# New ranks for the first 267 operations of a fused attention and feed-forward kernel, and the third block's loads behind the weights

## The chip, the cores and the metric

The kernel runs on one core of one Trainium2 chip. The metric is the time on the device in microseconds (us); several runs are made and their median is taken. One further execution was recorded by the hardware profiler, and everything that is read from a profile is read from that one.

## The reference

Linear attention, followed by a feed-forward layer with a sigmoid form of GELU. q, k and v are 8 x 8 x 576 x 64 (batch, heads, positions, width of a head); x has 4608 rows of 512; the weights are 512 x 2048 and 2048 x 512, handed over as 64-bit floats.

```python
q_s = exp(q - max(q, axis=-1)); q_s /= sum(q_s, axis=-1) + 1e-9
k_s = exp(k - max(k, axis=2));  k_s /= sum(k_s, axis=2) + 1e-9
kv  = einsum('bhsd,bhse->bhde', k_s, v)
x   = einsum('bhsd,bhde->bhse', q_s, kv)      # rows: batch and position, columns: head and width
h   = x @ w_in
out = (h / (1 + exp(-1.702 * h))) @ w_out
```

## The kernel before, in words

**Blocks.** The 4608 rows are cut into 12 blocks of 384 rows. A batch has 576 rows, so a block covers parts of one or two batches. For each block the kernel makes x (512 x 384, turned), then 16 steps j of the feed-forward part: `g1` multiplies 128 columns of w_in with x (12 products), ScalarE applies the GELU, and `g2` adds the result times 128 rows of w_out into three banks (three times three products). Each operand is held as a high part and a remainder (`h` and `l`), and three products replace one. The remainders (`xl`, `gl`, and the `l` half of a weight) are VectorE's work.

**Weights.** Each of 16 + 16 weight tiles (wi0 to wi15, wo0 to wo15, 512 KB each) is loaded once as 64-bit words and converted in place by `conv_w`: ScalarE scales the upper word (c1), VectorE shifts the lower word (c2, line 255), puts the words together in two integer steps (c3, lines 259 and 260), ScalarE casts the high part (c5, line 264) and VectorE subtracts it (c6, line 270). Three scratch tiles `tmp` go round, so that a conversion can begin only when the third one before it is done. The converted weights stay for all blocks.

**Attention.** For a new batch: `k_max` (VectorE, lines 397 to 399, then a maximum over partitions on GpSimd), `k_sub` (line 418, then the exponential on ScalarE), `kv_pairs` (products of k and v, then a division). For a block: `q_soft` (maximum and subtraction, lines 502 and 503; exponential, line 506; sum and division, lines 509 to 512), `q_tr` (turns q), `x_pairs` (q times kv) and `x_out` (high part on ScalarE, remainder xl on VectorE, line 547). Batches 0 and 1 are worked in two groups of four heads (i = 0, 1). For these two the inputs lie in the storage of weight tiles that are loaded later (`held`): the queries of batch 1, for example, in that of wi14 and wi15; such a weight's load waits until they are read.

**Steps.** Block 0 and block 1 share the weights as these come in: block 1's steps stand 9 ranks (`JOIN`) behind those of block 0. From block 2 on blocks follow each other, and the next block's attention lies between the steps of the one before.

**The order.** Nothing is ordered by hand. Every operation is handed to `Plan.add` with its engine, a cost in us, what it reads and writes, and a rank. `Plan.order` plays the plan through: whenever an engine is free, it takes, of the operations whose inputs are there by the estimates, the one with the lowest rank; it never leaves an engine idle for a better one. The program is written in the order in which the operations began there, and each engine then runs its own instructions in this order. All loads are issued on SyncE's queue. A load of so many bytes is expected by these lines:

```python
free[e] = done = now + cost
if size:
    wire = max(wire, done) + size / self.RATE
    done = wire + self.LAND
```

where `wire` is one line shared by all loads, `RATE` is in bytes per us, and `LAND` in us. `ISSUE` is the cost of an issue on SyncE.

Of the kernel before, what the change touches and what calls it, by code (L numbers as in the profile page):

```python
# [18 lines left out]
class Plan:  # L19
# [1 line left out]

    HOP, LAND, RATE, ISSUE, TABLE = 0.1, 1.8, 270e3, 0.5, 1.28

    def __init__(self):
        self.ops = []
# [19 lines left out]
    def order(self):  # L47
        ops = self.ops
        left = [len(o[2]) for o in ops]
        users = [[] for _ in ops]  # L50
        for n, o in enumerate(ops):
            for d in o[2]:
                users[d].append(n)
        engines = sorted({o[0] for o in ops})
        free = dict.fromkeys(engines, 0.0)
        ready = {e: [] for e in engines}
        coming = []
        at = [0.0] * len(ops)
        for n, o in enumerate(ops):
            if not left[n]:  # L60
                heapq.heappush(ready[o[0]], (o[3], n))
        wire, table = 0.0, None
        began = []
        self.start = {}
        now = 0.0
        while len(began) < len(ops):
            while coming and coming[0][0] <= now:
                _, n = heapq.heappop(coming)
                heapq.heappush(ready[ops[n][0]], (ops[n][3], n))
            moved = False  # L70
            for e in engines:
                if free[e] > now or not ready[e]:
                    continue
                _, n = heapq.heappop(ready[e])
                _, cost, _, _, _, needs, size = ops[n]
                if needs is not None and needs != table:
                    cost, table = cost + self.TABLE, needs
# [4 lines that stand above are left out]
                began.append(n)  # L82
                self.start[n] = now
                moved = True
                for u in users[n]:
                    left[u] -= 1
                    hop = 0.0 if ops[u][0] == e and not size else self.HOP
                    at[u] = max(at[u], done + hop)
                    if not left[u]:
                        heapq.heappush(coming, (at[u], u))  # L90
            if not moved:
                times = [f for e, f in free.items() if f > now and ready[e]]
                if coming:
                    times.append(coming[0][0])
                now = min(t for t in times if t > now) if any(t > now for t in times) else now
        return began


def dve(n, psum=False):
    return 0.15 + n / 960  # L100

# [6 lines left out]
def efficient_attention_then_gelu_ffn(  # L108
# [27 lines left out]
    ST = S - SM  # L136
    W = D + 1
    JOIN = 9

    const = ctx.enter_context(tc.tile_pool(name="const", bufs=1))  # L140
    psum = ctx.enter_context(tc.tile_pool(name="psum", bufs=1, space=bass.MemoryType.PSUM))
# [4 lines left out]
    def sb(name, shape, dtype=F32, tag=None):  # L146
        return const.tile(shape, dtype, name=name, tag=tag or name)
# [135 lines left out]
    def bc(a, n):  # L283
        return a.unsqueeze(len(a.shape)).broadcast_to([*a.shape, n])
# [4 lines left out]

    kbuf, vbuf, qbuf, tbuf = {}, {}, {}, {}  # L290

    def load_tail(b, rank):
        if b in etail:
            (kl, vl), tag = etail[b]
            keys = ((tag, 0), (tag, "v"))
        else:
            (kl, vl), keys = tail[0], ((("tail"), 0), (("tail"), 1))
        tbuf[b] = kl, vl, keys

        def run_k():  # L300
            nc.sync.dma_start(out=kl[0:ST], in_=k[b, :, SM:S, :].rearrange("h p d -> p h d"))  # L301

        def run_v():
            nc.sync.dma_start(out=vl[0:ST, :, 0:D], in_=v[b, :, SM:S, :].rearrange("h p d -> p h d"))  # L304

        plan.add("SP", plan.ISSUE, (), (keys[0],), rank, run_k, size=ST * H * D * 4)
        plan.add("SP", plan.ISSUE, (), (keys[1],), rank + 0.01, run_v, size=2 * ST * H * D * 4)

    def load_k(b, i, rank):
        n = group(b)  # L310
        t, key = ek[b, i] if b < 2 else (kt_[i], ("kt", i))
        kbuf[b, i] = t, key
        hs = slice(n * i, n * (i + 1))

        def run():
            nc.sync.dma_start(
                out=t.rearrange("p h c d -> p h (c d)"),
                in_=k[b, hs, 0:SM, :].rearrange("h (p c) d -> p h (c d)", c=CM),
            )

        plan.add("SP", plan.ISSUE, (), (key,), rank, run, size=n * SM * D * 4)

    def load_v(b, i, rank):
        n = group(b)
        t, key = ev[b, i] if b < 2 else (vt_[i], ("vt", i))
        vbuf[b, i] = t, key

        def run():
            if b < 2:
                nc.sync.dma_start(  # L330
                    out=t.rearrange("p h c d -> p h (c d)"),
                    in_=v[b, n * i : n * (i + 1), 0:SM, :].rearrange("h (p c) d -> p h (c d)", c=CM),
                )
                return
            for h in range(n):
                nc.sync.dma_start(
                    out=t[:, h, :, 0:D], in_=v[b, n * i + h, 0:SM, :].rearrange("(p c) d -> p c d", c=CM)
                )

        if b < 2:  # L340
            plan.add("SP", plan.ISSUE, (), (key,), rank, run, size=n * SM * D * 4)
        else:
            plan.add("SP", n * 0.6, (), (key,), rank, run, size=1.5 * n * SM * D * 4)

    def parts(t):

        t0 = t * TB
        b, s0 = divmod(t0, S)
        n = min(TB, S - s0)
        got = [(b, s0, 0, n // C)]  # L350
        if n < TB:
            got.append((b + 1, 0, n // C, P))
        return got
# [6 lines left out]
    def load_q(t, i, rank):  # L360
        n = group(t)
        qt, key = eq[t, i] if t < 2 else (qt_[i % 2], ("qt", i % 2))
        qbuf[t, i] = qt, key
        runs = [(0, 1, 1), (1, 0, 1)] if turned(parts(t)[0][0], i) else [(0, 0, n)]

        def run():
            for b, s0, p0, p1 in parts(t):
                for o, h, m in runs:
                    src = q[b, n * i + h : n * i + h + m, s0 : s0 + (p1 - p0) * C, :]
                    if t < 2:  # L370
                        nc.sync.dma_start(
                            out=qt[p0:p1].rearrange("p h c d -> p h (c d)"),
                            in_=src.rearrange("h (p c) d -> p h (c d)", c=C),
                        )
                    else:
                        nc.sync.dma_start(
                            out=qt[p0:p1, :, o : o + m], in_=src.rearrange("h (p c) d -> p c h d", c=C)
                        )

        plan.add("SP", plan.ISSUE * len(parts(t)) * len(runs), (), (key,), rank, run, size=n * TB * D * 4)  # L380

    nm = [0]
    maxes = {}
# [100 lines left out]

    nr = [0]
    rs = [sb(f"r{i}", [P, NP]) for i in range(2)]
    qm = [sb(f"qm{i}", [P, 4 * C]) for i in range(2)]

    def q_soft(t, i, ranks):
        n = group(t)  # L490
        qt, key = qbuf[t, i]
        M = ("qm", i % 2)
        dst, nkey = qt, key
        if t < 2:
            m = qm[i % 2].rearrange("p (h c) -> p h c", h=n)
            qn, nkey = qbuf[t, i] = en[t, i]
            dst = qn.rearrange("p c h d -> p h c d")
        else:
            m = qm[i % 2][:, : n * C].rearrange("p (c h) -> p c h", c=C)

        def run_m():
            nc.vector.tensor_reduce(out=m, in_=qt, axis=AX.X, op=ALU.max)  # L502
            nc.vector.tensor_tensor(out=qt, in0=qt, in1=bc(m, D), op=ALU.subtract)

        def run_e():
            nc.scalar.activation(qt, qt, AF.Exp)  # L506

        def run_s():
            nc.vector.tensor_reduce(out=m, in_=qt, axis=AX.X, op=ALU.add)  # L509
            nc.vector.tensor_scalar_add(m, m, 1e-9)  # L510
            nc.vector.reciprocal(m, m)
            nc.vector.tensor_tensor(out=dst, in0=qt, in1=bc(m, D), op=ALU.mult)

        e = n * C * D
        plan.add("DVE", 2 * dve(e), (key,), (key, M), ranks[0], run_m)
        plan.add("ACT", act(e), (key,), (key,), ranks[1], run_e, table="exp")
        plan.add("DVE", 2 * dve(e) + 0.35, (key,), (nkey, M), ranks[2], run_s)
# [234 lines left out]
    for rank, _, f, a in sorted(tasks, key=lambda s: s[:2]):  # L752
        if f in (load_k, load_v, load_q, k_max, k_sub, q_tr, x_pairs, g1, g2, load_w, conv_w, load_tail):
            f(*a, rank)
        else:
            f(rank)

    with tc.manual_schedule():
        for n in plan.order():
            plan.ops[n][4]()  # L760
# [24 lines left out]
```

## Time and profile before

| what | us |
|---|---|
| median of 3 runs (lowest, highest) | 916.12 (915.61, 918.11) |
| the profiled execution's own time | 916.58 |
| its span, first to last instruction | 914.7 |
| TensorE busy | 885.1 (97%) |
| VectorE busy | 390.2 (43%) |
| ScalarE busy | 487.8 (53%) |
| GpSimd busy | 27.8 (3%) |

The span is shorter than the execution's own time by what lies around the instructions. In the rows, PE is TensorE, PEld its weight loads, DVE VectorE, ACT ScalarE, POOL GpSimd and SP SyncE (SPq is its issuing of loads). L with a number is a line of the kernel. Tiles go by their names without numbers. PEclk is the TensorE clock that the chip granted, as a share of 2.4 GHz.

### The profile page before, as it was taken

How to read it: one execution, taken by the hardware profiler on the slowest of the kernel's cores; microseconds unless marked ns; L12 is line 12 of the kernel's file. 1: busy time of each engine (PE TensorE's matmuls, PEld its weight loads, DVE VectorE, ACT ScalarE, POOL GpSimd, SP SyncE). 2: the span in 40 equal slices, each digit the busy share in tenths (PEclk: the TensorE clock that was granted, in tenths of full speed). 3: DMA queues.
4: the chain of work that ended last, by engine and by line, in shares of the span. 5: the costliest groups of instructions: out<-in, count | busy, mean ns of one | idle time of the engine just before them, and what ended most of it. 6: DMA issues, size and time to landing. Idle time of an engine off the chain costs nothing.

```text
span 914.7 us, 13010 instructions
## 1 busy us (share of the span) xinstructions
PE 885.1 (97%) x5200; PEld 785.7 (86%) x5200; DVE 390.2 (43%) x826; ACT 487.8 (53%) x840; POOL 27.8 (3%) x35
## 2 busy tenths in 40 slices
PE   2879999999999999999999999999999999999998
PEld 2668989888988988989889889888988898998897
DVE  8899996162531641341541352332263134132111
ACT  3776669464952763552773583544494265253222
POOL 1100001000100100000000010000010000000000
PEclk9899999999999999999999999999999999999999
DMA  9996000111310400000400320000141000000000
GB/s 257 353 315 208 1 1 1 52 53 31 100 40 14 120 11 35 18 18 35 122 18 34 85 55 35 18 18 35 33 100 42 9 18 9 36 18 1 35 1 35
DMA packets 94620, 55.37 MB, mean 61 GB/s; under 512 B 67424, under 2 KB 87904, under 8 KB 94560
## 3 DMA queue, kind: packets, MB, share of 16 engines
q1 hardware_dynamic: 94560, 54.54, 21.0%
q8 instruction: 41, 0.67, 0.3%
q14 instruction: 19, 0.16, 0.1%
HBM read 45.09 MB, written 9.44 MB: 60 GB/s over the span
## 4 chain that ended last, share of the span: by engine, by line
PE 93%; DMA 4%; SPq 2%; DVE 1%; ACT 0%; issue 0%; DVEq 0%
PE bank L636 44%; PE bank L604 44%; PE bank L465 2%; PE bank L529 1%; PE bank L580 1%; DMA raw<-in_moe_w_out 1%; DMA raw<-in_moe_w_in 1%; DMA ek<-in_k 1%; SPq L226 0%; PE bank L575 0%; SPq L221 0%; DVE tmp L260 0%; SPq L304 0%; DVE tmp L259 0%; SPq L330 0%; SPq L301 0%
## 5 line engine op out<-in xcount | busy, mean ns | idle before, releaser
L604 PE MATMUL bank<-xh,w 128*128 128x384 f32 x1536 | 429.0, 341 | 4.6 <-ACT w L264 3.5
L636 PE MATMUL bank<-w,gh 128*128 128x512 f32 x1152 | 366.6, 399 | 0.0
L604 PEld LDWEIGHTS bank<-xh,w 128*128 128x128 f32 x1536 | 282.0, 189 | 14.7 <-ACT w L264 3.9
L616 DVE TENSOR_TENSOR gl<-g,gh 128x384 fp32r<-128x384 f32 x192 | 106.6, 556 | 385.0 <-ACT gh L613 384.3
L610 ACT ACTIVATE g<-bank 128x384 f32<-128x384 f32 x192 | 94.5, 492 | 326.8 <-PE bank L604 326.0
L604 PE MATMUL bank<-xl,w 128*128 128x384 f32 x768 | 259.7, 338 | 0.0
L636 PEld LDWEIGHTS bank<-w,gh 128*128 128x128 f32 x1152 | 214.5, 189 | 41.1 <-issue 4.4
L636 PE MATMUL bank<-w,gl 128*128 128x512 f32 x576 | 228.4, 397 | 0.0
L604 PEld LDWEIGHTS bank<-xl,w 128*128 128x128 f32 x768 | 144.9, 189 | 7.0
L636 PEld LDWEIGHTS bank<-w,gl 128*128 128x128 f32 x576 | 108.7, 189 | 25.8
L613 ACT CAST gh<-g 128x384 fp32r<-128x384 f32 x192 | 98.5, 513 | 6.3 <-PE bank L636 0.3
L610 ACT ACT_TABLE_LOAD x54 | 69.3, 1283 | 1.0
L502 DVE TENSOR_REDUCE qm<-qt 128x6 f32<-128x384 f32 x40 | 22.0, 551 | 67.2 <-DMA qt<-in_q 67.2
L506 ACT ACT_TABLE_LOAD x36 | 46.2, 1283 | 1.9 <-DMA qt<-in_q 1.3
L403 POOL PARTITION_ALL_REDUCE mx<-mx x24 | 21.0, 876 | 611.1 <-DVE mx L399 611.1
L536 ACT COPY qT<-bank 128x384 f32<-128x384 f32 x48 | 22.7, 476 | 29.8 <-PE bank L529 29.6
L509 DVE TENSOR_REDUCE qm<-qt 128x6 f32<-128x384 f32 x40 | 22.0, 550 | 25.7 <-ACT qt L506 25.6
L424 ACT ACT_TABLE_LOAD x18 | 23.1, 1283 | 5.5 <-DMA ek<-in_k 5.2
L465 PE MATMUL bank<-ev,ek 128*64 128x64 f32 x128 | 7.2, 273 | 19.0 <-ACT eq L506 12.4
L547 DVE TENSOR_TENSOR xl<-bank,xh 128x384 fp32r<-128x384 f32 x48 | 24.0, 550 | 3.0 <-ACT xh L544 3.0
L481 ACT ACTIVATE kvn<-bank,r 64x64 f32<-64x64 f32 x64 | 17.9, 306 | 14.0 <-DVE r L471 12.2
L251 ACT ACTIVATE tmp<-raw 128x512 f32<-128x512 f32 x32 | 21.2, 673 | 5.7 <-DVE w L270 5.6
(71 smaller groups left out, 495.4 us busy)
## 6 DMA issues: line engine op xcount, KB each, us to landing
out<-tmp SPq DMA_DIRECT2D x36, 256.0 KB, 2.1
raw<-in_moe_w_in SPq DMA_DIRECT2D x16, 512.0 KB, 10.0
raw<-in_moe_w_out SPq DMA_DIRECT2D x16, 512.0 KB, 10.2
kt<-in_k SPq DMA_DIRECT2D x24, 256.0 KB, 4.1
vt<-in_v SPq DMA_DIRECT2D x48, 128.0 KB, 4.0
qt<-in_q SPq DMA_DIRECT2D x36, 96.0 KB, 2.7
qt<-in_q SPq DMA_DIRECT2D x16, 192.0 KB, 2.9
ek<-in_k SPq DMA_DIRECT2D x4, 512.0 KB, 7.5
```

What stands on the lines that cost most here:

```text
L424: nc.scalar.activation(t, t, AF.Exp)
L465: nc.tensor.matmul(pk[r0 : r0 + D, m, cols], lhs, rhs, start=c == 0, stop=c == CM, tile_position=(0, r0))
L502: nc.vector.tensor_reduce(out=m, in_=qt, axis=AX.X, op=ALU.max)
L506: nc.scalar.activation(qt, qt, AF.Exp)
L509: nc.vector.tensor_reduce(out=m, in_=qt, axis=AX.X, op=ALU.add)
L536: nc.scalar.copy(qT, pq[:, :TB])
L547: nc.vector.tensor_tensor(out=xl, in0=px[:, :TB], in1=xh.bitcast(F32), op=ALU.subtract)
L604: nc.tensor.matmul(ph, wi[w][j][:, c, :], x[:, c, :], start=c == 0 and i == 0, stop=c == KC - 1 and i == 2,)
L610: nc.scalar.activation(gt, ph, AF.Gelu_apprx_sigmoid)
L613: nc.scalar.copy(gh, gt)
L616: nc.vector.tensor_tensor(out=gl, in0=gt, in1=gh.bitcast(F32), op=ALU.subtract)
L636: nc.tensor.matmul(po[c], x[:, cs], wo[w][j], start=j == 0 and i == 0, stop=j == NJ - 1 and i == 2)
```

## The change

Four edits. (1) The first 267 operations in the order of `add` with a rank under 12 get other ranks, from the table `FIRST`; all others keep theirs. The values were found by a search that played the plan through under five sets of estimates. (2) The planner's estimates of loads change: LAND from 1.8 to 2.2, RATE from 270e3 to 330e3, ISSUE from 0.5 to 0.6, and SyncE begins at 0.7. (3) `behind` makes the plan put every load of keys and values from batch 2 on, and of queries from block 2 on, behind the last write in the plan, at that point, of each tile that batch 1's inputs share with a weight. It is an order in the plan only: the buffers of these loads are others, and the chip waits for nothing more. (4) A second form of the queries' softmax with ScalarE's sums is added, for the groups named in `QACT`; the set is empty, so only its two small tiles are made.

```diff
-    HOP, LAND, RATE, ISSUE, TABLE = 0.1, 1.8, 270e3, 0.5, 1.28
+    HOP, LAND, RATE, ISSUE, TABLE = 0.1, 2.2, 330e3, 0.6, 1.28
...
-        free = dict.fromkeys(engines, 0.0)
+        free = dict.fromkeys(engines, 0.0) | {"SP": 0.7}
...
+FIRST = [
+    -3424, -9000, -8950, -8949, -8900, -8800, -8700, -8600, -8500, -8400, -8350, -8300, -8250, -8249, -8200, -8100,
+    -8000, -7900, -7800, -7899, -7123, -5395, -5792, -5064, 307, 3595, -4928, -4172, 1260, -5510, -5886, -124, 1298,
...
+]
...
+    QACT = set()
...
+    def behind(late):
+
+        return tuple((tag, 0) for tag, b in held.items() if b == 1) if late else ()
...
-        plan.add("SP", plan.ISSUE, (), (keys[0],), rank, run_k, size=ST * H * D * 4)
-        plan.add("SP", plan.ISSUE, (), (keys[1],), rank + 0.01, run_v, size=2 * ST * H * D * 4)
+        plan.add("SP", plan.ISSUE, behind(b > 1), (keys[0],), rank, run_k, size=ST * H * D * 4)
+        plan.add("SP", plan.ISSUE, behind(b > 1), (keys[1],), rank + 0.01, run_v, size=2 * ST * H * D * 4)
...
-        plan.add("SP", plan.ISSUE, (), (key,), rank, run, size=n * SM * D * 4)
+        plan.add("SP", plan.ISSUE, behind(b > 1), (key,), rank, run, size=n * SM * D * 4)
...
-            plan.add("SP", n * 0.6, (), (key,), rank, run, size=1.5 * n * SM * D * 4)
+            plan.add("SP", n * 0.6, behind(True), (key,), rank, run, size=1.5 * n * SM * D * 4)
...
-        plan.add("SP", plan.ISSUE * len(parts(t)) * len(runs), (), (key,), rank, run, size=n * TB * D * 4)
+        plan.add("SP", plan.ISSUE * len(parts(t)) * len(runs), behind(t > 1), (key,), rank, run, size=n * TB * D * 4)
...
+    sums = [sb(f"qs{i}", [P, 4 * C]) for i in range(2)]
...
+        if (t, i) in QACT:
...
+    begun = [n for n, o in enumerate(plan.ops) if o[3] < 12]
+    assert len(begun) == len(FIRST)
+    for n, r in zip(begun, FIRST):
+        e, cost, deps, _, run, table, size = plan.ops[n]
+        plan.ops[n] = e, cost, deps, r / 100, run, table, size
```

Counted off against the order of `add`, the ranks that the prediction speaks of are these (old, then new):

| operation | old | new |
|---|---|---|
| load of wi1, of batch 1's second values | -69, -78 | -78.99, -78.00 |
| load of wo3, of wi4 | -66.5, -66 | 3.07, 35.95 |
| k_max of batch 1, groups 0 and 1 | 0.4, 0.6 | -2.86, -1.23 |
| k_sub of batch 1, groups 0 and 1 | 0.5, 0.7 | -37.90, -105.52 |
| q_soft of block 1, maximum, groups 0 and 1 | 0.5, 0.7 | 0.13, -2.44 |
| q_soft of block 1, sum, groups 0 and 1 | 0.5, 0.7 | -4.46, 19.37 |
| exponentials of batch 1 and block 1 (k 0, q 0, q 1, k 1) | 0.5, 0.5, 0.7, 0.7 | -142.55, -51.56, -106.59, -78.98 |
| conversion of wi1: c2, c3, c6 | -0.2 | -73.63, -95.81, -8.94 |
| conversion of wo1: c2, c3, c6 | 0.3 | -35.20, -1.46, -58.90 |
| conversion of wi2: c2, c3, c6 | 1.8 | -4.45, -13.25, -94.43 |
| conversion of wo2: c2, c3, c6 | 2.3 | 17.40, -107.47, -51.11 |
| conversion of wi3: c2, c3, c6 | 3.8 | -33.74, -63.21, -49.11 |
| conversion of wo3: c2, c3, c6 | 4.3 | 43.23, -54.90, -1.24 |
| conversion of wi4: c2, c3, c6 | 5.8 | -82.61, 50.33, -67.93 |
| GELU of block 0, steps 0 to 3 | 0, 2, 4, 6 | -53.53, 42.80, -101.88, -48.65 |

## Rows read from the trace of the kernel before

**Rows 1.** Busy time of each engine in four stages (us from the start).

```profile
0.00:32.08 32.08, 15.43 (x180) 12.73 (x181) 25.00 (x57) 13.15 (x26) 3.64 (x10) 1.00 1.02 275
32.08:66.07 33.99, 25.13 (x247) 20.77 (x245) 31.68 (x60) 27.46 (x48) 3.17 (x2) 0.90 1.06 336
66.07:150.00 83.93, 83.93 (x414) 75.90 (x415) 79.06 (x149) 58.79 (x99) 4.08 (x4) 0.98 0.22 68
150.00:914.70 764.70, 760.64 (x4364) 676.34 (x4362) 254.45 (x564) 388.39 (x670) 16.93 (x20) 1.00 0.14 38
```

Columns of rows 1: the stretch and its length, then busy us and instructions of PE, PEld, DVE, ACT and POOL, then granted clock, share of the DMA engines, GB/s.

**Rows 2.** Timeline of TensorE from 32 to 67 us, the pieces after gaps.

```profile
36.06 0.69 PE L465 MATMUL bank<-ev,ek 128*64 128x64 f32 x16 [1.41 <-ACT ek L424]
...
39.68 0.51 PE L604 MATMUL bank<-xh,w 128*128 128x384 f32 x1 [1.11 <-ACT w L264]
...
41.14 1.01 PE L604 MATMUL bank<-xh,w 128*128 128x384 f32 x2 [0.64 <-DVE w L270]
...
52.74 0.69 PE L465 MATMUL bank<-ev,ek 128*64 128x64 f32 x16 [1.45 <-ACT ek L424]
...
65.06 0.45 PE L604 MATMUL bank<-xh,w 128*128 128x384 f32 x1 [2.42 <-ACT w L264]
...
66.07 0.62 PE L604 MATMUL bank<-xh,w 128*128 128x384 f32 x2 [0.38 <-DVE w L270]
```

Columns of a timeline: start and length in us, engine, line, operation, how many; in brackets the idle time ahead of it and what ended that.

**Rows 3.** Stretches of 2 us: TensorE's busy time and granted clock.

```profile
40.00:42.00 2.00, 1.36 (x5) 0.50 1.01 388
...
46.00:48.00 2.00, 2.00 (x9) 0.81 1.11 337
...
66.00:68.00 2.00, 1.93 (x9) 0.81 1.13 329
68.00:70.00 2.00, 2.00 (x7) 0.50 1.03 410
70.00:72.00 2.00, 2.00 (x9) 0.84 1.06 375
```

**Rows 4.** Timeline of VectorE from 30 to 66 us.

```profile
30.37 0.68 DVE L397 TENSOR_TENSOR em<-ek 128x512 f32<-128x512 f32 x1
...
37.02 0.42 DVE L255 TENSOR_SCALAR raw<-raw 128x512 uint32<-128x512 uint32 x1
37.55 0.70 DVE L259 SCALAR_TENSOR_TENSOR tmp<-tmp,raw 128x512 int32<-128x512 int32 x1
...
40.41 0.68 DVE L270 TENSOR_TENSOR w<-tmp,w 128x512 fp32r<-128x512 f32 x1
...
60.15 0.42 DVE L255 TENSOR_SCALAR raw<-raw 128x512 uint32<-128x512 uint32 x1
...
64.86 0.55 DVE L547 TENSOR_TENSOR xl<-bank,xh 128x384 fp32r<-128x384 f32 x1
65.33 0.68 DVE L270 TENSOR_TENSOR w<-tmp,w 128x512 fp32r<-128x512 f32 x1
```

**Rows 5.** Chain of waits from 0 to 75 us: two loads.

```profile
12.92 9.76 DMA ek<-in_k
...
26.76 11.87 DMA raw<-in_moe_w_out
```

**Rows 6.** Timeline of SyncE's issues.

```profile
42.04 4.36 SPq L376 DMA_DIRECT2D qt<-in_q  x2
...
73.89 3.39 SPq L226 DMA_DIRECT2D raw<-in_moe_w_out  x1
```

**Rows 7.** Timeline of VectorE: the first maximum of block 2.

```profile
134.44 0.55 DVE L502 TENSOR_REDUCE qm<-qt 128x6 f32<-128x384 f32 x1
```

**Rows 8.** What ScalarE waited for from 30 to 150 us: the longest.

```profile
ACT g L610 <- PE bank L604: 15.3, 17, 2.5
```

**Rows 9.** Timeline of ScalarE: a table load and what follows it.

```profile
36.34 1.28 ACT L610 ACT_TABLE_LOAD   x1
37.63 0.49 ACT L610 ACTIVATE g<-bank 128x384 f32<-128x384 f32 x1
```

More of the change, by code (lines that the diff above doesn't have):

```diff
@@ L514, in q_soft, with run_n, run_a, run_z @@
         e = n * C * D
+        if (t, i) in QACT:
+            flat = qt.rearrange("p h c d -> p (h c d)")
+            mf, sf = qm[i % 2], sums[i % 2]
+            def run_n():
+                nc.vector.tensor_reduce(out=m, in_=qt, axis=AX.X, op=ALU.max, negate=True)
+            def run_a():
+                for x in range(n * C):
+                    w = flat[:, x * D : (x + 1) * D]
+                    nc.scalar.activation(w, w, AF.Exp, bias=mf[:, x : x + 1], accum_out=sf[:, x : x + 1])
+            def run_z():
+                nc.vector.tensor_scalar_add(sf, sf, 1e-9)
+                nc.vector.reciprocal(sf, sf)
+                nc.vector.tensor_tensor(
+                    out=dst, in0=qt, in1=bc(sf.rearrange("p (h c) -> p h c", h=n), D), op=ALU.mult
+                )
+            Q = ("qs", i % 2)
+            plan.add("DVE", dve(e), (key,), (M,), ranks[0], run_n)
+            plan.add("ACT", 0.30 * n * C, (key, M), (key, Q), ranks[1], run_a, table="exp")
+            plan.add("DVE", dve(e) + 0.4, (key, Q), (nkey, Q), ranks[2], run_z)
+            return
         plan.add("DVE", 2 * dve(e), (key,), (key, M), ranks[0], run_m)
```

15 rows, old and new, of the table FIRST are left out of this document.

## Prediction

> **What bounds the kernel now.** I read the page first, then the busy time by stage, then each engine's timeline of the first 72 us. The four stages hold 15.43 + 25.13 + 83.93 + 760.64 = 885.13 us of TensorE work in 914.7 [rows 1], so what the change can give lies in the few stretches where it stands still. The stage table says where these are: from 66.07 us to 150 us TensorE has no idle time, and from 150 us to the end 4 us in 764.7. The first 32.08 us hold 15.43 us of busy time, the next 33.99 us hold 25.13. So 8.86 us of idle time lie between the first matmul of the feed-forward part (32.08) and 66.07, and 16.65 before it. The first part is the start of the chain: first loads, softmax of block 0, its small products. The second is where the new ranks can act most.
>
> In that second part the timeline gives the gaps one by one; the six largest that the change can touch are 1.41, 1.11, 0.64, 1.45, 2.42 and 0.38 us [rows 2]. Two of them (1.11 and 0.64) are the second step of the first layer, which waits for the conversion of wi1; the last two (2.42, 0.38) are its fourth step, which waits for wi3. Behind the gaps the granted clock falls to its lower level, 1.2 instead of 2.4 GHz [rows 3]: from 40 to 46 us it is 0.50 (the two stretches between 42 and 46 read as the one shown) and to 48 us 0.81, which costs 3 x 1.0 + 0.38 = 3.4 us, some 0.3 of which is gap counted already; from 66 to 72 us 0.81, 0.50, 0.84, that is 0.38 + 1.0 + 0.32 = 1.7. Gaps and clock make about 8.9 + 3.1 + 1.7 = 13.7 us; no more than this can come out of the second part.
>
> VectorE is what feeds it: 31.68 us busy of 33.99 [rows 1]. Its order in that time is a mix of two things [rows 4]: the softmax work of block 1 (from 30.37, last remainder x low at 64.86) and the weights' conversions. wi1 gets its first conversion step at 37.02 and its last at 40.41; wi3 its first at 60.15 and its last at 65.33.
>
> **The change, part by part.**
>
> *The planner's estimates.* The planner thought of loads as slower than they are. Up to the second key load of batch 1 it counts 5.77 MB; at 270 kB per us, plus 0.5 and 1.8, it expects that load at 23.7 us, and by the new constants (330 kB per us, plus 1.3 and 2.2) at 21.0. The chain of waits has it land at 12.92 + 9.76 = 22.68. For wo3 (10.75 MB) the two estimates are 42.1 and 36.1, and it lands at 26.76 + 11.87 = 38.63 [rows 5]. The truth lies between: the old plan was 1 to 3.5 us late, the new one is 1.7 to 2.6 us early. That matters in two ways. A late estimate makes the planner put other work first: wi1 was expected at 0.5 + 8.13/0.27 + 1.8 = 32.4, so block 1's maxima (30.37) and subtractions went ahead of it although its old rank (-0.2) stood before theirs (0.4). An early estimate puts a step in the queue ahead of work that could run while its load still travels.
>
> *wi1 earlier (gain).* Its load moves ahead of block 1's second value load, and its integer steps get ranks -73.63 and -95.81, far below block 1's maxima (-2.86) and softmax (0.13). By the new estimate it is there at 26.5. From the two landings the chip moves 4.98 MB in 15.95 us, 312 kB per us, so 7.60 MB are there at 22.68 + 1.84/0.312 = 28.6. Its steps cost on VectorE 0.42 + 0.70 + 0.70 + 0.68 [rows 4], the second integer step being as long as the first, so wi1 is whole by some 36 to 37 instead of 41.09. Then the second step of the first layer follows the first at once: the gaps 1.11 and 0.64 go, and the 1.41 ahead of them, in which TensorE had nothing else, is filled: 3.2 us. The clock's fall from 40 to 47 hangs on these gaps; but further on TensorE still waits for wi2 and for block 1, so I count half of it, 1.5. Cost: the integer steps of wi1 (0.42 + 1.40) now run ahead of the last remainders of block 0, which is 1.8 us on the first step of the first layer, and VectorE stands up to 1.0 us for the load (28.6 against the some 27.5 at which its queue gets there). Sum: 3.2 + 1.5 - 2.8 = 1.9 us gained. Bounds: 0 (the clock falls anyway, the stall is 2) to 4.7 (the clock stays, no cost on the path).
>
> *wi3 ahead of wo2, wo3 and of block 1's last softmax (gain).* Its steps get -33.74, -63.21 and -49.11; the gate of wo2 gets 17.40, that of wo3 43.23 and the last sum of block 1 (group 1) 19.37. So wi3 is converted before block 1 is ready, and the fourth step of the first layer waits no more: 2.42 + 0.38, and the fall of the clock behind it, 1.7. Sum 4.5 us. Bounds: 2.8 (the clock falls elsewhere) to 4.5.
>
> *What VectorE does ahead of block 1's end (loss).* The old order ran six whole conversions and two half ones (wi3, wo3) before 64.86. By the ranks the new one runs seven (wi0 to wi3, wo0 to wo2) and the gate of wo4 or wi4. So block 1 is ready at about the time it was, and the gaps that are filled are filled with steps of block 0 (the first layer's fourth step, 2.1, the second layer's third). After them TensorE has nothing until block 1 comes, since the last softmax sum stands so late: a new gap, taken as 1.5 (0 to 3; nearest row the 1.45 in which TensorE waits for a piece of block 1 now [rows 2]). And wi3 is planned at once on its estimated landing, which the chip misses by 1.7 to 2.6: 1.4 us of VectorE standing still (0 to 2.6), with all of block 1 queued behind it.
>
> *Third block's loads behind the weights (nothing).* These are two q, four k and eight v loads, 2.75 MB with the tails, now between the weights from 42.04 on; the last weight is issued at 73.89 [rows 6]. Behind them, they are issued at about 70 to 80 us. VectorE first needs them at 134.44 [rows 7], and no conversion after 66 us waits for a load: ScalarE, which makes each first step, waits most for TensorE (15.3 us), and what it waits for after 30 us is always another engine, never a load [rows 8]. So weights that come 8 us earlier (2.75 MB at the 336 GB/s of that stage [rows 1]) bring nothing, and the cover of some 50 us would have to go before the move costs. The edit of the planner that is not used (the set of softmax groups on ScalarE is empty) is nothing either; its two small tiles cost no time.
>
> *Table loads.* The new ranks mix the GELU of block 0 (-53.53, 42.80, -101.88, -48.65) with the exponentials of block 1 (-142.55, -51.56, -106.59, -78.98). Six table loads stand in the first 65 us now; the new order has about as many, two more at worst. One costs 1.28 us: the load starts at 36.34 and the GELU at 37.63 [rows 9]. The Trainium skill, ScalarE: Activation LUTs, section "What ACT_TABLE_LOAD costs", puts a switch at 2.66 us, a drain included, and advises to do all work of one set first; by it two more switches would cost 5.3 us. The trace shows no drain beside the 1.28 here.
>
> **Sum.** -1.9 - 4.5 + 1.5 + 1.4 = -3.5 us. The profiled execution took 916.58 us (span 914.7 and 1.88 around it), so 913.1; it lies 0.46 above the median of the runs, and on the median's scale the forecast is 916.12 - 3.5 = 912.6 us. From 0.3% (2.75 us) on a difference can be told from none here, so this is a little more than the least that counts.
>
> **Rivals.**
>
> *Nothing moves (chance 0.27, 914 to 918).* VectorE has 31.68 of 33.99 us of work [rows 1] and the change takes none of it away; if block 1's end stays and the clock falls as often, what the two gaps give is lost in the new one. For it: the same number of conversions ahead of block 1. Against: the gaps at wi1 and wi3 are of order, not of amount. Time: -1.9 - 2.8 + 3 + 2 = +0.3, so 916.4.
>
> *Loads later than the plan (slower; chance 0.15, 919 and up).* Each engine runs its instructions in the one order that the plan wrote down; each conversion that the plan starts on its estimated landing stands until the chip's. Five weights (wi1, wo1, wi2, wo2, wi3) land within this time. If all of them are met up to 2.6 us early and block 1's work stands behind, the stalls add to 5 x 1.7 = 8.5 less the 1.0 and 1.4 counted: +6.1 - 3.5 = +2.6, so 918.7. It decides once four of the five stalls lie on VectorE's path. Against it: after one stall the queue is itself late, and the next load has time.
>
> *The clock stays up (chance 0.12, 907 to 910).* If no gap over 1.5 us is left after 32 us, gaps and clock come back nearly whole: 4.7 + 4.5 - 1.4 (the stall at wi3) = 7.8, so 908.3.
>
> *Table switches (within the second-largest chance, 0.04 of its own).* Two more, 2 x 1.28 = 2.6 us on ScalarE, ahead of block 1's casts: 912.6 + 2.6 = 915.2. In a sentence by itself: by the Trainium skill's 2.66 each it would be 917.9.
>
> **Chances.** The forecast's own case (2 to 6 us faster, 910 to 914) has 0.42, the large gain 0.12, nothing 0.27 and the switches 0.04, slower 0.15. Of the forecast's case some 0.01 ends above 913.4, so faster 0.53, same 0.32, slower 0.15. The range leaves out some 0.05 below and 0.15 above: 908.5 to 918.5; the forecast's own is 910 to 914.
>
> **What the new profile would show.** Right: wi1's last conversion step before 38 us and the second step of the first layer directly behind the first; no wait for wi3 at 65; one clock fall instead of two; TensorE without gaps from some 62 to 64 us on; third block's loads issued behind the last weight with nothing waiting for them. Wrong: VectorE idle on weight loads between 27 and 40 us (the second rival), block 1's last remainder later than 66 us, more than eight table loads ahead of 65 us, or gaps after 66 us, where now there are none.

## The result: 904.8 us, and the profile of the changed kernel

The changed kernel takes 904.77 us in the median of 4 runs (903.55 to 905.83), the kernel before 915.87 (915.45 to 918.11) in the same set of runs: a ratio of 0.9869 (95%: 0.9855 to 0.9883), 11.1 us less. The profiled execution took 903.99 us, its span is 902.2. The direction was forecast, the size was not: 3.5 us were expected, and 904.77 lies below the range.

The four stages of the profile after, with the columns of [rows 1]:

```profile
0.00:32.08 32.08, 16.62 (x187) 13.84 (x187) 26.98 (x59) 15.11 (x30) 4.69 (x10) 1.00 1.02 294
32.08:66.07 33.99, 29.88 (x273) 26.09 (x273) 32.54 (x64) 25.89 (x48) 1.30 (x1) 0.90 1.07 375
66.07:150.00 83.93, 83.93 (x425) 75.93 (x424) 75.49 (x143) 58.36 (x99) 2.75 (x3) 1.00 0.17 45
150.00:902.20 752.20, 748.15 (x4320) 666.98 (x4318) 252.50 (x561) 401.95 (x677) 15.87 (x21) 1.00 0.14 39
```

Against [rows 1], TensorE's idle time went from 16.65 to 15.46 us in the first stage and from 8.86 to 4.11 in the second: 1.2 and 4.75 us. The clock of the second stage is 0.90 in both; in the third it was 0.98 and is 1.00 (84 x 0.02 = 1.7 us). Together 7.6 of the 12.5 us by which the spans differ. (The two recordings lie further apart than the medians, 12.6 against 11.1 us.) The rest doesn't come out of idle time at all; the first experiments say where it lies.

TensorE's timeline from 32 to 67 us, every piece with idle time ahead of it, answers to [rows 2]:

```profile
34.55 0.44 PE L659 MATMUL bank<-xl,w 128*128 128x384 f32 x1 [2.45 <-DVE xl L602]
...
36.77 1.12 PE L494 MATMUL bank<-ev,ek 128*64 128x64 f32 x16 [0.60 <-ACT ek L453]
...
48.46 0.87 PE L584 MATMUL bank<-ident,en 128*128 128x128 f32 x6 [0.19 <-DVE en L542]
49.58 1.57 PE L630 MATMUL bank<-qT,kvn 128*128 128x192 f32 x8 [0.24 <-ACT qT L591]
...
58.71 0.85 PE L584 MATMUL bank<-ident,en 128*128 128x128 f32 x6 [0.64 <-DVE en L542]
```

The gaps at wi1 (1.11, 0.64) and at wi3 (2.42, 0.38) are gone. One large gap is new, 2.45 us in the middle of the first layer's first step: TensorE waits there for a remainder of block 0. VectorE's timeline shows why (it answers to [rows 4]):

```profile
29.75 0.95 DVE L532 TENSOR_REDUCE qm<-eq 128x12 f32<-128x768 f32 x1
...
31.62 0.42 DVE L280 TENSOR_SCALAR raw<-raw 128x512 uint32<-128x512 uint32 x1
32.14 0.69 DVE L284 SCALAR_TENSOR_TENSOR tmp<-tmp,raw 128x512 int32<-128x512 int32 x1
32.87 0.69 DVE L285 SCALAR_TENSOR_TENSOR tmp<-raw,tmp 128x512 int32<-128x512 int32 x1
33.48 1.01 DVE L602 TENSOR_TENSOR xl<-bank,xh 128x384 fp32r<-128x384 f32 x2
...
36.82 0.67 DVE L295 TENSOR_TENSOR w<-tmp,w 128x512 fp32r<-128x512 f32 x1
...
48.32 0.42 DVE L280 TENSOR_SCALAR raw<-raw 128x512 uint32<-128x512 uint32 x1
...
51.98 0.68 DVE L295 TENSOR_TENSOR w<-tmp,w 128x512 fp32r<-128x512 f32 x1
...
63.02 1.20 DVE L602 TENSOR_TENSOR xl<-bank,xh 128x384 fp32r<-128x384 f32 x2
```

A maximum and a subtraction of block 1 (from 29.75) and then wi1's gate (its first step on VectorE, c2) and integer steps (31.62 to 33.5) stand ahead of block 0's last two remainders. wi1 is whole at 37.5. wi3's gate is at 48.32 instead of 60.15 and its last step at 51.98, ahead even of wi2's (53.05). Block 1's last remainder ends at 64.2 instead of 65.4, with eight whole conversions ahead of it (wi0 to wi3, wo0 to wo3) where the order before had six and two halves. No bracket of VectorE names a load between 6 and 66 us, and none names a weight's load in the whole run: it never stood on a weight. In the stretch from 5 to 66 us it was busy for 56.23 us (53.38 before): its idle brackets between 23 and 66 us add up to 1.5 us, where before they were 1.46, 0.87 and 0.72 up to 30 us and 0.90 and 0.26 behind.

The clock, in stretches of 2 us, answers to [rows 3]:

```profile
34.00:36.00 2.00, 1.45 (x5) 1.12 (x5) 2.00 (x5) 0.61 (x2) 0.00 (x0) 0.74 1.03 403
36.00:38.00 2.00, 1.40 (x25) 1.23 (x24) 2.00 (x4) 1.98 (x3) 0.00 (x0) 0.50 1.06 356
38.00:40.00 2.00, 2.00 (x25) 1.99 (x24) 1.63 (x5) 1.75 (x5) 0.00 (x0) 0.50 1.10 349
40.00:42.00 2.00, 2.00 (x9) 2.00 (x8) 1.93 (x5) 1.96 (x4) 0.94 (x1) 0.55 1.10 349
42.00:44.00 2.00, 2.00 (x45) 1.74 (x44) 1.97 (x3) 1.29 (x3) 0.37 (x1) 1.00 1.06 399
```

It falls once, behind the 2.45 us gap, and comes back at some 42 us after TensorE had worked on without idle time from 36.8; the second fall [rows 3] is gone, with the gap ahead of it.

On SyncE's queue the third block's loads stand behind the last weight, and block 2's first maximum ([rows 7]) is the first of VectorE's work on them:

```profile
59.59 1.12 SPq L251 DMA_DIRECT2D raw<-in_moe_w_out  x1
60.76 4.49 SPq L405 DMA_DIRECT2D qt<-in_q  x2
```

```profile
129.38 0.55 DVE L532 TENSOR_REDUCE qm<-qt 128x6 f32<-128x384 f32 x1
```

### The profile page after: what moved, and what is told of

Read it like the earlier page. It is cut to its first block, busy times and chain, and to the rows that moved or that the text cites. A ratio compares the mean times of both kernels' runs of the same rounds, so it can differ in the third digit from the quotient of the medians.

```text
span 902.2 us, 13027 instructions
## 1 busy us (share of the span) xinstructions
PE 878.6 (97%) x5200; PEld 782.8 (87%) x5200; DVE 387.5 (43%) x826; ACT 501.3 (56%) x850; POOL 24.6 (3%) x35
## 4 chain that ended last, share of the span: by engine, by line
PE 94%; DVE 4%; ACT 1%; DMA 0%; issue 0%; POOL 0%; ACTq 0%; DVEq 0%
PE bank L691 44%; PE bank L659 44%; PE bank L494 2%; PE bank L584 2%; PE bank L635 1%; PE bank L630 1%; DVE ek L447 1%; DMA ek<-in_k 0%; DVE en L542 0%; DVE eq L533 0%; DVE tmp L284 0%; DVE tmp L285 0%; DVE qm L539 0%; DVE qm L532 0%; ACT ek L453 0%; DVE em L426 0%
## 5 line engine op out<-in xcount | busy, mean ns | idle before, releaser
L432 POOL PARTITION_ALL_REDUCE mx<-mx x24 | 18.6, 776 | 603.8 <-DVE mx L428 603.8
L289 ACT CAST w<-tmp 128x512 fp32r<-128x512 f32 x32 | 19.5, 618 | 14.2 <-DVE tmp L285 11.0
```

## The experiments

All times are medians, beside the median of the kernel before on the same chip in the same set of runs (915.76 to 917.17). Every run has a ratio to that kernel with its 95% interval. Where two changed kernels are compared, their medians are, mostly from different sets; by the intervals such a difference is known to some 2 us, so that one of 1 or 1.5 us can be told from none only with other evidence.

### Where are the 4.9 us that no idle time explains?

The long stage holds, by its groups, 2025 + 1539 products of the two layers before and 1999 + 1521 after: 26 and 18 fewer, for the stages ahead did more. At 2.12 us for 12 and 2.11 for 9 that is 4.6 + 4.2 = 8.8 us, yet the stage is 12.5 us shorter: about 3.7 us come from the same steps being quicker. TensorE's steps follow in nearly the same order there. The chain of waits from 540 to 600 us shows single steps, first of before, then of after:

```profile
557.17 2.12 PE bank L604 x12
559.28 2.09 PE bank L636 x9
561.37 2.12 PE bank L604 x12
563.49 2.11 PE bank L636 x9
```

```profile
554.78 2.09 PE bank L659 x12
556.87 2.09 PE bank L691 x9
```

What the diff changes for all steps alike is only where tiles lie: the two unused `qs` tiles take 128 bytes of each partition ahead of the weights that share no storage with the early inputs (wi0 to wi4, wi11, wi12, wo0 to wo6). So: the tiles into the kernel before, and out of the changed one.

```diff
+    sums = [sb(f"qs{i}", [P, 4 * C]) for i in range(2)]     # b_two_tiles: added to before
-    sums = [sb(f"qs{i}", [P, 4 * C]) for i in range(2)]     # a_no_tiles: taken out of after
```

> The kernel before with nothing but the two unused tiles of the new softmax form, which move every weight tile that shares no storage with an early input by 128 bytes. Placement theory (the 3.7 us that the changed kernel gains after 150 us come from where those weights lie): steps of the first layer fall from 2.12 to 2.09 us, time 911 to 913 us. Order theory (they come from the order of later operations): steps stay at 2.12, time 916 us within 1.

> The changed kernel without those two tiles. Placement theory: steps of the first layer return to 2.12 us, time 908 to 909.5 us. Order theory: 904.8 us within 1.

Measured: before with the tiles 912.93 (0.9958, 0.9945 to 0.9971), 3.6 us faster; after without them 907.98 (0.9906, 0.9892 to 0.9921), 3.2 us slower than the 904.77 with them. Two tiles that nothing reads give 3.2 to 3.6 us, and the rest of the change (ranks, estimates and `behind`) gives 912.93 - 904.77 = 8.2, called the order's part below.

Then a shift by another amount, 32 bytes, in both:

```diff
+    pad = sb("pad", [P, 8])
```

> The changed kernel with one more unused tile of 32 bytes, so that those weights begin at a multiple of 64 bytes, as the weights in shared storage do. Placement theory: all steps of the first layer at 2.08 us, time 902.5 to 904 us. Order theory: 904.8 us within 1.

> The kernel before with that tile of 32 bytes alone. Placement theory: steps at 2.08, time 910 to 912 us. Order theory: 916 us within 1.

Measured: after 904.06 (0.9866, 0.9850 to 0.9882), no change; before 913.08 (0.9959, 0.9945 to 0.9973), as quick as with 128 bytes. Both missed the times expected of the placement theory (902.5 to 904, 910 to 912), which looked at the first layer alone. So it is neither the tiles nor the size of a shift. In the first the steps with shifted weights take 2.12 in the first layer, longer than after's 2.09, and some 2.07 in the second, less than after's 2.09: gains and losses cancel. I set the times against the addresses, counted off from the order and size of the tiles in a partition (each rounded up to 32 bytes; no trace shows an address), modulo 256. What fits all of them is the distance of the moving operand from the stationary one. In the first layer (stationary wi, moving x at 128) wi at 32, 64, 160 and 192 took 2.12, 2.08, 2.09 to 2.10 and 2.12 us a step; in the second (stationary g at 128, moving wo) wo at 32, 64, 160 and 192 took 2.10 to 2.11, 2.09 to 2.11, 2.08 to 2.10 and 2.07. Distance 64 is the quickest in both.

That can be tried: lay the storage out so that every wi lies at 64 and every wo at 192, x and g staying at 128 (the order is left as it is in after; the core of the edit):

```diff
+    for j in range(NJ):
+        if j not in (10, 13):
+            place(f"wi{j}")
     em, _ = early("wi13", "em", [P, 4 * 4 * D], 1)
+    qm = [sb(f"qm{i}", [P, 4 * C]) for i in range(2)]
+    for j in range(NJ):
+        place(f"wo{j}")
+    rs = [sb(f"r{i}", [P, NP]) for i in range(2)]
+    sb("gap", [P, 16])
```

> The changed kernel with all weights' storage laid out by hand: every wi tile begins 64 bytes past a multiple of 256, every wo tile 192 past, order and work as they were. In the runs so far steps of the first layer were quickest (2.08 us) with 64 and those of the second (2.07) with 192. If the place alone sets a step's time: all first-layer steps at 2.08 and second-layer steps at 2.07 us, 899 to 902 us. If it was the place of a tile among its neighbours or something else that shifted with it: 904.8 us within 1.5.

Measured: 898.81 (0.9800, 0.9783 to 0.9818), 6 us below the changed kernel, the fastest of the study. Its steps in the chain of waits from 540 us on:

```profile
544.28 2.08 PE bank L673 x12
546.36 2.07 PE bank L705 x9
```

Two more tell the distance from the address: everything moved by 128 bytes (distances kept), and only x and g moved by 128 while the weights move by 256 (distance 192 in both layers).

```diff
+    sb("shift", [P, 32])                          # a_shift_all: ahead of the first tile
...
+    rs = [sb(f"r{i}", [P, NP]) for i in range(2)] # a_shift_moving: these as well,
+    sb("gap", [P, 16])                            # moved ahead of the weights
```

> The kernel with placed weights (898.8 us), everything from the first tile on moved by 128 bytes. If the distance between the two operands of a product sets its time: steps stay at 2.08 and 2.07 us, 898.8 us within 1. If the weights' own address sets it: 2.12 and 2.10 us, 904 to 908 us.

> The same kernel with x, the GELU's tiles and all else ahead of the weights moved by 128 bytes and the weights by 256, so that only the distance between the operands changes. If the distance sets the time: steps of 2.12 and 2.10 us, 904 to 908 us. If the weights' own address modulo 256 sets it: 898.8 us within 1.

Measured: 899.31 (0.9822, 0.9806 to 0.9839) and 909.81 (0.9936, 0.9921 to 0.9951). The steps of the second:

```profile
550.07 2.12 PE bank L674 x12
552.18 2.09 PE bank L706 x9
```

Moving both operands by 128 bytes changes nothing (898.81 and 899.31); moving one against the other does: 10.5 us between distance 64 and 192, more than the 904 to 908 expected. The other tiles ahead of the weights moved together with x and g, so the distance to one of them isn't ruled out by these two runs alone; that the two layers answer to distances of opposite sign (x - wi, wo - g) speaks for the operands. From the steps, 192 x (0.04 + 0.02) = 11.5 would be expected for the 192 pairs of steps in the program. The same sum gives the two tiles: 7 of 16 weights a layer, 84 x (0.03 + 0.02) = 4.2 against the 3.2 to 3.6 measured, as near as steps read to 0.01 us allow.

### Which part of the change gives the other 8.2 us?

First the estimates by themselves (LAND, RATE, ISSUE and SyncE's start): the new ones in before, with the two tiles so that 912.93 is the measure, and the old ones in after.

```diff
-    HOP, LAND, RATE, ISSUE, TABLE = 0.1, 1.8, 270e3, 0.5, 1.28   # b_new_estimates; the reverse: a_old_estimates
+    HOP, LAND, RATE, ISSUE, TABLE = 0.1, 2.2, 330e3, 0.6, 1.28
```

> The kernel before with the two unused tiles (so that the weights lie as in the changed kernel; 912.9 us) and the planner's new estimates of loads, old ranks. If the late estimates were what held wi1 and block 1 back: most of the 8 us between 912.9 and 904.8 come, 905 to 908 us. If the search's ranks carry the gain: 912.9 us within 1.5.

> The changed kernel with the planner's old estimates of loads, new ranks kept. If the ranks carry the gain whatever the estimates: 904 to 907 us. If ranks and estimates only work together: 909 us or more.

Measured: 911.70 (0.9943, 0.9925 to 0.9961), 1.2 below 912.93, and 906.13 (0.9882, 0.9864 to 0.9900), 1.4 above 904.77. The estimates are worth about 1.3 us, which can't be told from none; the ranks, with `behind`, carry the gain. The first of the two kernels shows more than its time. In it VectorE takes wi1's gate at 34.08 instead of 37.02, ahead of block 1's subtraction, and wi1 is whole at 38.5 instead of 41.1: the late estimate did hold wi1 back, as the prediction said. But the wait only moves. TensorE stands 4.21 us for block 1's softmax instead:

```profile
34.08 0.42 DVE L255 TENSOR_SCALAR raw<-raw 128x512 uint32<-128x512 uint32 x1
```

```profile
49.32 1.54 PE L530 MATMUL bank<-ident,en 128*128 128x128 f32 x6 [4.21 <-DVE en L513]
```

Then single ranks: wi3's gate back behind block 1's last softmax, and wi1's gate to 0.50, just above its old rank of -0.2. Among the new ranks, most of which are far below zero, 0.50 is not its old place: wi1 comes much later than it did before, as VectorE's timeline shows below.

```diff
-    for n, r in zip(begun, FIRST):
+    first_ranks = list(FIRST)
+    first_ranks[172] = 2100      # a_wi3_late: gate of wi3, was -3374
+    first_ranks[98] = 50         # a_wi1_late, in place of it: gate of wi1, was -7363
+    for n, r in zip(begun, first_ranks):
```

> The changed kernel with one rank altered: the first conversion step of wi3 from -33.74 to 21.00, behind the last softmax sum of block 1, so that wi3 is whole some 5 us later. Prediction's step (wi3's place is worth 2.8 to 4.5 us): 907.5 to 909.5 us, with a gap ahead of the first layer's fourth step. Rival (TensorE has other work by then): 904.8 us within 1.

> The changed kernel with one rank altered: the first conversion step of wi1 from -73.63 to 0.50, behind block 1's maxima. Prediction's step (wi1's place is worth 1.9 us, 0 to 4.7): 905 to 909.5 us, 906.7 likeliest, with gaps ahead of the second step of the first layer. Rival (wi1's place is nothing by itself): 904.8 us within 0.8.

Measured: wi3 late 908.07 (0.9905, 0.9887 to 0.9923), 3.3 slower than after; wi1 late 909.74 (0.9921, 0.9903 to 0.9939), 5.0 slower. With wi1 late, wi1's gate and its last step stand here on VectorE:

```profile
50.85 0.42 DVE L280 TENSOR_SCALAR raw<-raw 128x512 uint32<-128x512 uint32 x1
...
56.63 0.68 DVE L295 TENSOR_TENSOR w<-tmp,w 128x512 fp32r<-128x512 f32 x1
```

So wi1 is whole at 57.3, 16 us later than before (41.1) and 20 later than in after (37.5), and the 5.0 us are the price of that, not of the 3.6 us that the change moved it. TensorE's timeline:

```profile
33.40 0.44 PE L659 MATMUL bank<-xl,w 128*128 128x384 f32 x1 [0.36 <-DVE xl L602]
...
44.63 0.69 PE L659 MATMUL bank<-xh,w 128*128 128x384 f32 x1 [1.89 <-ACT w L289]
46.73 1.01 PE L659 MATMUL bank<-xh,w 128*128 128x384 f32 x2 [1.10 <-DVE w L295]
```

The 2.45 us gap of after is 0.36 here, so most of that gap is the price of wi1's early steps. The 3.0 us of waiting at 42 to 47 are for wi2, whose step the plan now takes second (its last conversion step ends at 46.7); wi1's own step comes at 58.15, without a wait. The second stage:

```profile
32.08:66.07 33.99, 26.64 (x248) 22.42 (x247) 31.94 (x62) 25.71 (x48) 1.06 (x1) 0.80 1.07 374
```

TensorE has 3.2 us less work done in it than in after, and a clock of 0.80 instead of 0.90. With wi3 late (its gate at 60.90, as late as before) the same stage reads:

```profile
32.08:66.07 33.99, 29.97 (x259) 25.94 (x258) 31.29 (x60) 25.35 (x47) 1.31 (x1) 0.80 1.07 375
```

There TensorE is as busy as in after. What is worse in this recording is a start 1.3 us later (15.28 us busy up to 32.08 instead of 16.62), the clock, 0.29 us of waiting for wi3 and 0.6 us of idle time after 66.07. The first two can't be the work of the rank. Up to wi3's gate, at 48.32 in after, all engines run the same instructions in the same order in both kernels; the late start is a load of the first queries that landed later (9.48 without a wait in after):

```profile
10.73 0.95 DVE L532 TENSOR_REDUCE qm<-eq 128x12 f32<-128x768 f32 x1 [1.25 <-DMA eq<-in_q]
```

and the clock, which fell behind the same gap (2.47 here), came back at some 50 us instead of 42. The recording is also the slowest of the kernel's four runs (909.60), with a granted clock of 0.992 over the whole span; the other three had 0.994 to 0.996. One of these had 0.996 and 907.72 us, and the three runs of after at 0.996 had 903.99, 905.55 and 905.83. So wi3's place is worth something like 2 to 3 us by the medians and these runs, but the recording shows only 0.9 of it as waits.

Then the new ranks for VectorE's operations alone, the old ones for all other engines:

```diff
     for n, r in zip(begun, FIRST):
+        if plan.ops[n][0] != "DVE":
+            continue
```

> The changed kernel with the new ranks for VectorE's operations alone; TensorE, ScalarE, GpSimd and SyncE keep the old ones. If VectorE's order carries the gain: 904 to 906.5 us. If the ranks only fit together: 907.5 us or more.

Measured: 908.96 (0.9916, 0.9894 to 0.9937), 4.0 below 912.93. This kernel also has the new estimates and `behind`, so the 4.0 us are not VectorE's ranks alone; the other 4.2 need the ranks of the other engines, which were found together with them.

### The loads behind the weights

Last the one part that was forecast at nothing: the changed kernel with `behind` giving no dependence.

```diff
-        return tuple((tag, 0) for tag, b in held.items() if b == 1) if late else ()
+        return ()
```

> The changed kernel with the third block's loads left free to go between the weights. Prediction's step (nothing): 904.8 us within 1. Rival (2.75 MB ahead of the early weights hold wi2, wi3 up by up to 8 us): 906 to 910 us, with VectorE waiting for weight loads before 60 us.

Measured: 909.11 (0.9915, 0.9898 to 0.9933), 4.3 us slower. VectorE's timeline of this kernel:

```profile
60.71 0.53 DVE L532 TENSOR_REDUCE qm<-qt 128x6 f32<-128x384 f32 x1
61.28 0.56 DVE L533 TENSOR_TENSOR qt<-qt,qm 128x384 f32<-128x384 f32 x1
...
66.47 0.54 DVE L539 TENSOR_REDUCE qm<-qt 128x6 f32<-128x384 f32 x1
```

That is block 2's softmax, 69 us ahead of its place in after (129.38), in the middle of the conversions. By the planner's rule it was taken there because its queries were there by the estimates and nothing of a lower rank was ready. Its ranks are those it had before (33.80 and 34.55 for the two maxima), while `FIRST` gives some early steps ranks above them: the gate of wo3 43.23 instead of 4.3, an integer step of wi4 50.33 instead of 5.8. So block 2's work now passes ahead of these. TensorE then stands in the next stage, which was full in after (33.93 of 33.93):

```profile
66.07:100.00 33.93, 31.57 (x153) 26.95 (x154) 32.79 (x63) 22.28 (x40) 0.00 (x0) 1.00 0.48 163
```

Is it the loads or the softmax? In the next kernel the loads keep their free places among the weights, and the plan puts block 2's softmax and the later batches' maxima behind the weights instead.

```diff
-        plan.add("SP", plan.ISSUE, behind(b > 1), (keys[0],), rank, run_k, size=ST * H * D * 4)
+        plan.add("SP", plan.ISSUE, (), (keys[0],), rank, run_k, size=ST * H * D * 4)
...
-        plan.add("DVE", 2 * dve(e), (key,), (key, M), ranks[0], run_m)
+        plan.add("DVE", 2 * dve(e), (key, *behind(t > 1)), (key, M), ranks[0], run_m)
```

> The changed kernel with the third block's loads free among the weights, as in the run without the edit (909.1 us), but with the softmax and the maxima of these later blocks put behind the weights in the plan instead. If the edit is worth its 4.3 us because it keeps block 2's softmax out of VectorE's queue before 70 us: 904.8 us within 1. If it is worth them because the loads hold the weights up: 908 to 910 us.

Measured: 905.44 (0.9874, 0.9859 to 0.9890), 0.7 from after and within its spread. The loads among the weights cost nothing that these runs can tell; the work they make ready costs the 3.7 to 4.3 us.

## Why the prediction was wrong, point by point

**"Its two small tiles cost no time."** The step that failed first. They cost none on any engine, but they move the storage of 14 weights and so the duration of the products with these weights all through the program. 3.2 to 3.6 us of the 11.1 are from there. The prediction looked for gains in idle time alone and took a product's duration as given.

**"What VectorE does ahead of block 1's end (loss)", 1.5 + 1.4.** The second step that failed, and it had the wrong sign. The pieces of block 1 waited 1.10, 1.45 and 0.34 us before (two of them in [rows 2]) and 0.19, 0.24 and 0.64 after: 1.8 us gained instead of 2.9 lost. Of the new gap "taken as 1.5" the 0.64 is what there is; of the "1.4 us of VectorE standing still" on wi3 there is nothing. The prediction took VectorE as full from its 31.68 of 33.99 us in the second stage, so that an eighth conversion could only push block 1 back. But VectorE had stood idle for 3.05 us between 23 and 30 us, and 1.2 behind; the new order leaves 1.5 in all, and did eight conversions and block 1's end 1.2 us sooner. The loss by loads was reckoned from an estimate of the landing that is too early; yet no weight was late for VectorE's queue. ScalarE's first step waited once for a weight, 2.6 us for wi0 at 14.89, and no experiment prices that wait. The rival of late loads fell with this.

**wi1 earlier, "1.9 us gained, bounds 0 to 4.7".** Right in its parts, near the lower bound in its sum. Of the gaps 1.41, 1.11 and 0.64 only 0.60 is left, wi1 was whole at 37.5 (before 38 was forecast), and the cost on the first step is there as a gap of 2.45 against the 2.8 counted. That is 3.2 gone and 3.05 come, 0.1 us gained by the gaps; and the half of the clock's fall that was counted as a gain (1.5) did not come, for the stage's clock is 0.90 in both. No run prices this term: the run with wi1 late puts wi1 at 57.3, not at 41.1, and the new estimates alone bring wi1 forward and lose the gain again at block 1.

**wi3 ahead, "4.5 us, 2.8 to 4.5".** The waits of 2.42 and 0.38 and the second fall of the clock are gone, as forecast, 4.5 us by the rows. Undone by itself the rank costs 3.3 us by the medians, inside the bounds, but it does not bring the 2.42 back, for the ranks around it are new too.

**Not in the sum: the first stage.** 1.2 us less idle time; the feed-forward part begins at 30.41 instead of 32.08. No experiment separated what of this is the order and what the landing of the first loads; the recording with wi3 late shows that a landing alone can shift the start by 1.3 us.

**"Third block's loads behind the weights: nothing."** Wrong as the price of the edit, which is worth 4.3 us given the new ranks, though the reason given (VectorE doesn't need them before 134 us) is true. It looked at the old plan, in which block 2's softmax stood at 134.44 with its loads free among the weights [rows 7], and did not set the new ranks of early steps (43.23, 50.33) against those of block 2. This is no part of the 7.6 us by which the forecast was missed: the forecast, like the changed kernel, has block 2's softmax where it was.

**Table loads.** Four ahead of 65 us instead of six, and 118 instead of 108 in the whole run, each 1.28 us by the page. The Trainium skill, ScalarE: Activation LUTs, "What ACT_TABLE_LOAD costs", gives 2.66 us for a switch, by which ten more would be 26.6 us of ScalarE, an estimate. No part of that shows in this program's time: TensorE's idle time after 150 us is 4.06 us before and 4.05 after.

**The clock.** One fall instead of two, as forecast; the rival in which it stays up did not come: it fell behind the 2.45 us gap. That rival's time, 908.3, was passed by other means.

In sum, by the rows: 0.1 (wi1) + 4.5 (wi3 and the clock) + 1.8 (block 1) = 6.4 us in the second part where 3.5 were forecast, 1.2 in the first stage and 3.2 to 3.6 from placement, together 10.8 to 11.2 against the 11.1 measured. This is an account of gaps, not a test of each. The runs show the two large parts (3.2 to 3.6 placement, 8.2 order) and that the order's part is not the sum of its pieces: 5.0 (wi1, put later than it ever was), 3.3 (wi3), 4.3 (`behind`) and 1.4 (estimates) make 14.0, each undone alone in a plan made for the others.

## What to carry to other kernels

When a change touches storage, compare the duration of the same steady step before and after before looking for waits: a few hundredths of a microsecond in 168 of 384 steps were a third of this gain, and laying operands out on purpose gave 6 us more. In a planned order that never idles, ask of each load not only who waits for it but what work it makes ready, and whether the rank of that work lets it pass ahead of what is urgent. Before a run with one rank put back is read as that operation's price, look up where the operation came to stand. A stall or gap forecast from an estimated landing is worth counting only if the queue ahead of it would be on time.

## What the runs showed of the hardware that was not expected

The duration of a matmul of these types (128 x 128 stationary, 384 or 512 columns of fp32r) depends on the distance of its moving from its stationary operand within a partition, counted here modulo 256 bytes (a longer period is not ruled out). Of the distances that occurred, 64 was quickest (2.08 us for 12 products of 384 columns, 2.07 for 9 of 512), 192 took 2.12 and 2.09 to 2.11, 96 and 160 (one layer each) 2.12 and 2.10 to 2.11, 224 and 32 (one layer each) 2.09 to 2.10 and 2.08 to 2.10. Over the program it is 899.31 against 909.81 us, with the order of operations the same. Other distances were not tried, and why it is so stays open.

The clock's return is not explained by these runs either. In after it came back at some 42 us behind work without a gap from 36.8 on. In the recording with wi3 late TensorE worked without a gap from 38.1 on, in the same order, and the clock stayed at 0.50 for about 8 us more:

```profile
40.00:42.00 2.00, 2.00 (x13) 1.99 (x12) 1.60 (x6) 1.74 (x5) 0.00 (x0) 0.50 1.10 349
...
48.00:50.00 2.00, 2.00 (x6) 1.52 (x6) 1.90 (x5) 1.99 (x5) 0.00 (x0) 0.53 1.10 349
50.00:52.00 2.00, 2.00 (x11) 1.59 (x10) 1.93 (x4) 0.08 (x1) 0.00 (x0) 1.00 1.10 348
```

Nor does PEclk tell the rate everywhere. In the kernel before, 16 products of 64 columns took 1.12 us here, in a stretch (12 to 26 us) whose granted clock reads 1.00:

```profile
12.44 1.12 PE L465 MATMUL bank<-ev,ek 128*64 128x64 f32 x16 [12.44 <-ACT eq L506]
```

The same 16 took 0.69 us at 36.06 [rows 2], where it also reads 1.00, and 1.12 us at 36.77 in after, where it reads 0.50. So a part of TensorE's busy time ahead of 26 us is at the slower rate in both kernels, which the account above leaves out.
